# Block-sparse attention and a gated MLP in one kernel: scores by 512 and 256 columns, and five preparation steps moved to later slots

## The chip, the cores and the metric

The kernel runs on one core of a Trainium2 chip. The core has five engines with instruction streams of their own: TensorE (PE in the profile; its weight loads are PEld) for matrix products and transposes, VectorE (DVE), ScalarE (ACT), GpSimd (POOL) and SyncE (SP), which here issues DMAs. Each engine works through its stream in order and waits at semaphores. TensorE writes to PSUM, eight banks of 2 KB in each partition; GpSimd doesn't read PSUM in this kernel. The metric is the device time of one execution in microseconds, the median over runs.

## The reference

Attention over 4 batches, 8 heads, 768 positions and 64 dimensions a head, with a mask of 24 x 24 blocks of 32 positions (a band, the first and last row and column of blocks, and three sampled blocks in each row), then a gated MLP on the joined heads:

```python
scores = scale * np.matmul(q, k.transpose(0, 1, 3, 2))
...
scores = np.where(mask, scores, -1000000000.0)
scores = scores - np.max(scores, axis=-1, keepdims=True)
attn = np.exp(scores)
attn = attn / (np.sum(attn, axis=-1, keepdims=True) + 1e-09)
return np.matmul(attn, v).astype(np.float32)
...
h = np.maximum(x @ w_in, 0.0)
u, v = (h[..., :d_ff // 2].copy(), h[..., d_ff // 2:].copy())
...
v_n = (v - mu) / np.sqrt(var + 1e-06)
v_s = np.einsum('ts,bsd->btd', w_spatial, v_n) + b_spatial[None, :, None]
gated = u * v_s
return (gated @ w_out).astype(np.float32)
```

Here `x` is 4 x 768 x 512, `w_in` 512 x 1024, `w_spatial` 768 x 768 and `w_out` 512 x 512. The inputs are float32; the kernel computes its products in bfloat16.

## The kernel before

*The mask inside the product.* The tile `kq` holds, for eight heads at a time, K transposed (columns 0 to 767) and Q transposed (columns 768 to 1535) in partitions 0 to 63. Partitions 64 to 87 (`MR`) hold 24 block rows: on the K side a one where the column belongs to that block, on the Q side 0 or a large negative number for each (block, query). One product over 88 partitions gives score plus mask, transposed: keys in partitions, queries in columns. `mask_rows` makes the Q-side block rows for one third of the queries (256 columns) by a product of `bm` with the K-side rows of head 0 and a copy into head 0's rows; `rows` copies the rows of head 0 to other heads.

*Slots.* The program is written as a list of slots (`for s in range(NS + LAG + 2)`), and the engines' streams follow that order; nothing is reordered later. Each slot issues one score tile of 128 keys (four parts for a unit) with its exponential on ScalarE, into one of two PSUM tiles `sc` of two banks each. Then come the functions of `pre`, the products of the exponentials with V that are due (tags `av`, two banks), the functions of `at`, some steps of the MLP from a queue (`run_queue`), and the functions of `late`.

Slots 0 to 35 (batch 0) work in units of a third of the queries and a pair of heads (`qk_unit`, L395 and L400; `av_unit`, L441), so that work can begin before all of Q is there. Heads 0 and 1 come first with two thirds at once, then pairs 1 to 3 with the first third, pairs 1 to 3 with the second (from slots 15, 18 and 21 on), and all four pairs with the last (from slots 24, 27, 30 and 33 on). Slots 36 to 179 (batches 1 to 3) take one head and one tile of 128 keys against all 768 queries (`qk_full`, L408 and L412; `av_full`, L459).

*Preparation for batch 0.* K and Q arrive in natural layout, are cast by GpSimd, and are transposed on TensorE (L261) into a PSUM bank, from which VectorE copies them into `kq` (L209). `tr_first(p)` does K and the first third of Q for pair p; `tr_rest(p)` the rest of Q: four transposes and two copies of 64x512. The block rows of heads 1 to 7 are copies of `rows` on VectorE or GpSimd (L239). All of these hang in the slots' lists; `ROWS` names slot, first head, last head and columns for those on VectorE.

*The shared banks.* Two single PSUM banks, `moeA` and `moeB`, are handed out in turn by `moe_tag`: to `mask_rows`, to `tr_first` and `tr_rest`, to the transposes of the attention's result for pair 0 (`xtr_third(1)`, at the end of slot 13), and to each product of the MLP. A user of a bank can start when the copy out of it by the user before the last has ended. The MLP of batch 0 begins at slot 16 (`open_first`): one step, a product of 512 columns (L545), and keeps that bank until slot 20. The results of the other units are transposed into the unused end of their own `av` tile (`xtr_third`, at slots 14, 15, 19 and so on), and copied out to `xt`; the tile can then be used for the unit after the next.

*GpSimd* works through the casts of the inputs and weights (L135, L225) in the order of `ORDER`, which stands in its stream ahead of all slots; `rows(slice(1, 4), qcols(2), PL)` of slot 16 follows.

Of the kernel before, what the change touches and what calls it, by code (L numbers as in the profile page):

```python
# [10 lines left out]
FP32 = mybir.dt.float32  # L11
BF16 = mybir.dt.bfloat16
I32 = mybir.dt.int32
AF = mybir.ActivationFunctionType
# [12 lines left out]
def kernel(  # L27
# [16 lines left out]
    nc = tc.nc  # L44

    B, H, S, D = q.shape
# [4 lines left out]
    HALF = S // 2  # L51
# [19 lines left out]
    psum = ctx.enter_context(tc.tile_pool(name="psum", bufs=1, space=bass.MemoryType.PSUM))  # L71
# [10 lines left out]
    kq = const.tile([KR, H, 2 * S], BF16, name="kq")  # L82
# [5 lines left out]
    def qcols(t0, n=1):  # L88
        return slice(S + t0 * TW, S + (t0 + n) * TW)
# [144 lines left out]
    def rows(hs, cs, eng=nc.vector):  # L234
        src = kq[MR, 0:1, cs].to_broadcast([NB, hs.stop - hs.start, cs.stop - cs.start])
        if eng is nc.scalar:
            nc.scalar.activation(out=kq[MR, hs, cs], in_=src, func=AF.Copy)
        else:
            eng.tensor_copy(out=kq[MR, hs, cs], in_=src)  # L239
# [11 lines left out]
    def moe_tag():  # L251
        moe_tags.rotate(1)
        if moe_tags[0] in held:
            moe_tags.rotate(1)
        return moe_tags[0]
# [10 lines left out]
    def mask_rows(ps, t, copy, h=0):  # L266
        nc.tensor.matmul(out=ps[:, 0:TW], lhsT=bm, rhs=kq[:, h, t * TW:(t + 1) * TW],
                         start=True, stop=True)
        copy(kq[MR, 0, qcols(t)], ps[0:NB, 0:TW])
# [103 lines left out]
    a_ref, av_ref, x_ref, xn_ref, xt_ref = {}, {}, {}, {}, {}  # L373
# [28 lines left out]
    def qk_full(j, ci):  # L402
        if ci == 0:
            a_ref["h", j] = work.tile([128, NCH * S], BF16, tag="a_all", bufs=3,
                                      name="a_all").rearrange("p (c n) -> p c n", c=NCH)
        ps = psum.tile([128, 1024], FP32, tag="sc", bufs=2)
        for hf in range(2):
            nc.tensor.matmul(out=ps[:, hf * 512:hf * 512 + HALF],  # L408
                             lhsT=kq[:, j % H, ci * 128:(ci + 1) * 128],
                             rhs=kq[:, j % H, S + hf * HALF:S + (hf + 1) * HALF],  # L410
                             start=True, stop=True)
        nc.scalar.activation(  # L412
            out=a_ref["h", j][:, ci, :].rearrange("p (b c) -> p b c", b=2),
            in_=ps.rearrange("p (b c) -> p b c", b=2)[:, :, 0:HALF], func=AF.Exp, scale=0.125)

    def av_tile(key, n):
        ps = psum.tile([128, 512], FP32, tag="av", bufs=2, name="ps_av")
# [277 lines left out]
    at, late, pre = {}, {}, {}  # L695

    def when(slot, *fns):
        at.setdefault(slot, []).extend(fns)

    def c(f, *a, **kw):  # L700
        return lambda: f(*a, **kw)

    K_Q0 = slice(0, S + TW)
    ROWS = [(3, 2, 8, qcols(0)), (1, 3, 4, K_), (4, 4, 6, K_), (8, 6, 8, K_),
            (14, 4, 8, qcols(1, 2))]
    when(0, second)
    when(1, third)
    when(2, lambda: filler(FILL3, psum.tile([128, 512], FP32, tag=moe_tag(), bufs=1, name="wps")))
# [1 line left out]
        when(sl, c(tr_first, p))  # L710
    for sl, h0, h1, cs in ROWS:
        when(sl, c(rows, slice(h0, h1), cs))
    when(3, lambda: mask_rows(psum.tile([128, 512], FP32, tag=moe_tag(), bufs=1, name="mq"), 2, dve_copy))
    when(16, lambda: rows(slice(1, 4), qcols(2), PL))
    for p, sl in ((1, 11), (2, 13), (3, 15), (0, 18)):
        when(sl, c(tr_rest, p, 2 if p == 0 else 1))
    for u, slot in enumerate((13, 14, 15, 19, 22, 25, 28, 30, 34, 37, 40), 1):
        (pre if u == 2 else late).setdefault(slot, []).append(c(xtr_third, u))
# [94 lines left out]
    for s in range(NS + LAG + 2):  # L813
        if s < S0:
            qk_unit(*divmod(s, 3))
        elif s < NS:
            j, ci = divmod(s - S0, NCH)
            qk_full(j + H, ci)
        early = at.get(s, [])
        for f in pre.get(s, []):  # L820
            f()
        for u, e in av_at.get(s, []):
            av_unit(u, e)
        if 0 <= s - LAG - S0 and s - LAG < NS:
            j, qc = divmod(s - LAG - S0, NCH)
            av_full(j + H, qc)
        for f in early:
            f()
        run_queue()
        for f in late.get(s, []):  # L830
            f()
        while post:
            post.pop(0)()
# [31 lines left out]
```

## Time and profile before

| | us |
|---|---|
| median of 3 runs | 211.86 (211.82 to 212.51) |
| the profiled execution | 211.45 |
| its span, first to last instruction | 209.4 |
| TensorE busy | 203.5 (97%) |
| ScalarE busy | 168.7 (81%) |
| VectorE busy | 131.5 (63%) |
| GpSimd busy | 85.0 (41%) |

A row of a timeline gives the start, the duration, the engine, the line, and the operation with what it writes and reads, and in brackets the idle time of the engine before it and what ended that. Rows of one line that follow each other are merged (x4). A matmul's duration has a tail in it that lies under the next one, so for TensorE the distance from start to start is the cost, and a wait can hide in a duration. A row of busy time by stretch gives the stretch, its length, then for PE, PEld, DVE, ACT and POOL the busy time and the number of instructions, the granted clock of TensorE, the mean share of the DMA engines and GB/s.

### The profile page before, as it was taken

The numbers are of one execution on the slowest core, as the hardware profiler recorded it, in microseconds if no ns is written. First come the engines' busy times: TensorE is split into PE (matmuls) and PEld (weight loads), VectorE is DVE, ScalarE is ACT, GpSimd is POOL, SyncE is SP. The second block draws the span as 40 slices with busy tenths as digits, with TensorE's granted clock in tenths as the row PEclk, the third lists the DMA queues.
The fourth block names the chain that finished last, engine by engine and source line by source line (L and its number), as shares of the span: only waits on it lengthen the run. The fifth ranks groups of instructions, "written<-read, shape, count | busy, mean of one in ns | idle before, by whom it ended". The sixth has DMA issues, their size and how long they took to land.

```text
span 209.4 us, 5342 instructions
## 1 busy us (share of the span) xinstructions
PE 203.5 (97%) x2140; PEld 129.3 (62%) x2140; DVE 131.5 (63%) x292; ACT 168.7 (81%) x221; POOL 85.0 (41%) x184
## 2 busy tenths in 40 slices
PE   7899999999999999999999999999999999999993
PEld 6698877756666666656555665565665556544441
DVE  7899776989654455594965464284984443476551
ACT  6999999999989999978898888989899787266021
POOL 7888869886919615007068061006220000012000
PEclk9999999999999999999999999999999999999999
DMA  5999899999999989689955697488401225510256
GB/s 156 349 360 349 272 328 271 240 315 354 277 305 191 280 239 250 227 212 366 172 186 113 153 220 170 173 187 254 83 3 38 50 53 121 214 56 2 50 146 229
DMA packets 64684, 41.96 MB, mean 200 GB/s; under 512 B 45716, under 2 KB 59412, under 8 KB 64660
## 3 DMA queue, kind: packets, MB, share of 16 engines
q1 hardware_dynamic: 64228, 41.24, 75.8%
q10 hardware_dynamic: 432, 0.39, 0.6%
q8 instruction: 16, 0.26, 0.5%
q14 instruction: 8, 0.07, 0.1%
HBM read 24.38 MB, written 6.29 MB: 146 GB/s over the span
## 4 chain that ended last, share of the span: by engine, by line
PE 90%; ACT 5%; DMA 2%; DVE 1%; issue 0%; ACTq 0%; POOL 0%
PE ps_moe L545 33%; PE ps L408 22%; PE ps_av L459 13%; PE ps_t L545 7%; PE ps L395 5%; ACT a_all L400 4%; PE ps_av L441 4%; PE ps_sc L545 3%; DMA st_q<-in_q_dram 1%; DMA out_dram<-osb 1%; PE ps L261 1%; PE ps_av L261 1%; DVE kq L209 0%; ACT osb L212 0%; DVE xt L209 0%
## 5 line engine op out<-in xcount | busy, mean ns | idle before, releaser
L412 ACT ACTIVATE a_all<-ps 128x768 bf16<-128x768 f32 x144 | 113.8, 812 | 15.8 <-PE ps L408 7.2
L408 PE MATMUL ps<-kq 88*128 88x384 bf16 x288 | 70.5, 325 | 0.0
L459 PEld LDWEIGHTS <-a_all 128*128 128x128 bf16 x864 | 46.4, 97 | 20.0
L459 PE MATMUL ps_av<-vv,a_all 128*128 128x65 bf16 x864 | 51.2, 194 | 0.0
L408 PEld LDWEIGHTS <-kq 88*128 88x128 bf16 x288 | 28.0, 98 | 30.2 <-issue 0.2
L545 PE MATMUL ps_moe<-w_in_t,xt 128*128 128x512 bf16 x144 | 43.8, 378 | 0.0
L400 ACT ACTIVATE a_all<-ps 128x1024 bf16<-128x1024 f32 x36 | 34.6, 1027 | 1.1 <-PE ps L395 0.8
L135 POOL CAST nat<-st_k 128x256 bf16<-128x256 f32 (+3 forms) x37 | 16.6, 481 | 43.4 <-DMA st_k<-in_k_dram 30.6
L545 PE MATMUL ps_moe<-vn,w_spt 128*128 128x512 bf16 x108 | 32.7, 378 | 0.0
L613 DVE SCALAR_TENSOR_TENSOR un<-ps_moe,b_col,un 128x512 bf16<-128x512 f32 x18 | 13.5, 749 | 17.1 <-PE ps_moe L545 16.9
L582 POOL TENSOR_SCALAR std<-mv 128x3 f32<-128x3 f32 (+1 forms) x9 | 2.2, 240 | 50.3 <-DVE mv L579 37.0
L395 PE MATMUL ps<-kq 88*128 88x256 bf16 (+1 forms) x140 | 21.5, 275 | 1.0 <-ACT a_all L400 0.6
L545 PE MATMUL ps_moe<-w_out_t,gt 128*128 128x512 bf16 x72 | 21.5, 378 | 0.0
L423 DVE RECIPROCAL rc<-ps_av 128x6 f32<-128x6 f32 (+1 forms) x36 | 6.6, 185 | 20.7 <-PE ps_av L459 18.9
L135 POOL CAST vv<-st_v 128x256 bf16<-128x256 f32 (+1 forms) x36 | 18.1, 534 | 3.8 <-DMA st_v<-in_v_dram 3.8
L545 PEld LDWEIGHTS <-xt 128*128 128x128 bf16 x192 | 15.2, 97 | 7.0 <-DVE xt L209 0.2
L424 DVE TENSOR_TENSOR xn<-ps_av,rc 128x384 bf16<-128x384 f32 (+1 forms) x36 | 18.5, 513 | 1.2
L135 POOL CAST nat<-st_q 128x256 bf16<-128x256 f32 (+2 forms) x41 | 18.1, 472 | 0.9 <-DMA st_q<-in_q_dram 0.6
L578 DVE BATCH_NORM_STATS2 stats<-vn 128x6 f32<-128x512 bf16 x24 | 16.5, 688 | 1.5 <-ACT vn L573 0.9
L183 DVE TENSOR_SCALAR vn<-ps_moe 128x512 bf16<-128x512 f32 x18 | 12.3, 684 | 6.0 <-PE ps_moe L545 6.0
L395 PEld LDWEIGHTS <-kq 88*128 88x128 bf16 x140 | 12.6, 97 | 4.7 <-issue 0.9
L209 DVE COPY kq<-tt 64x1536 bf16<-64x1536 bf16 x24 | 14.9, 619 | 0.3
(86 smaller groups left out, 210.1 us busy)
## 6 DMA issues: line engine op xcount, KB each, us to landing
st_v<-in_v_dram SPq DMA_DIRECT2D x16, 384.0 KB, 6.0
out_dram<-osb SPq DMA_DIRECT2D x23, 256.0 KB, 2.4
st_k<-in_k_dram SPq DMA_DIRECT2D x15, 384.0 KB, 4.4
st_q<-in_q_dram SPq DMA_DIRECT2D x12, 384.0 KB, 4.2
ws_f<-in_moe_w_spatial_dram SPq DMA_DIRECT2D x6, 384.0 KB, 5.0
w_f<-in_moe_w_in_dram SPq DMA_DIRECT2D x8, 256.0 KB, 6.3
w_f<-in_moe_w_out_dram SPq DMA_DIRECT2D x4, 256.0 KB, 5.3
st_q<-in_q_dram SPq DMA_DIRECT2D x3, 256.0 KB, 6.6
```

What stands on the lines that cost most here:

```text
L135: eng.tensor_copy(out=dst, in_=src)
L183: nc.vector.tensor_scalar(out=out, in0=in0, scalar1=s1, scalar2=s2, op0=o0, **kw)
L209: nc.vector.tensor_copy(out=o, in_=i)
L395: nc.tensor.matmul(out=ps[:, at:at + n * TW], lhsT=kq[:, h, ci * 128:(ci + 1) * 128], rhs=kq[:, h, qcols(t0, n)], start=True, stop=True)
L400: nc.scalar.activation(out=out, in_=ps, func=AF.Exp, scale=0.125)
L408: nc.tensor.matmul(out=ps[:, hf * 512:hf * 512 + HALF], lhsT=kq[:, j % H, ci * 128:(ci + 1) * 128], rhs=kq[:, j % H, S + hf * HALF:S + (hf ...
L412: nc.scalar.activation(out=a_ref["h", j][:, ci, :].rearrange("p (b c) -> p b c", b=2), in_=ps.rearrange("p (b c) -> p b c", b=2)[:, :, 0:H ...
L424: nc.vector.tensor_tensor(out=out, in0=ps[:, :, 0:D], in1=rc[:, 0:n].to_broadcast([128, n, D]), op=ALU.mult)
L459: nc.tensor.matmul(out=av_ref[j][:, qc, :], lhsT=a_ref["h", j][:, ci, qc * 128:(qc + 1) * 128], rhs=vv[p % NVV][:, h, ci, :], start=(ci == ...
L545: nc.tensor.matmul(out=ref["ps"][:, 0:w], lhsT=lhs(i), rhs=rhs(i), start=(i == 0), stop=(i == n - 1))
L578: nc.vector.bn_stats(out=stats, in_=self.vn[:, tcc, :])
L613: nc.vector.scalar_tensor_tensor(out=self.un[:, tcc, :], in0=ps, scalar=b_col[:, tcc:tcc + 1], in1=self.un[:, tcc, :], op0=ALU.add, op1=AL ...
```

## The change

`qk_full` splits its 768 columns into 512 and 256 instead of two halves of 384 in two banks; the scores then lie next to each other in PSUM, and the exponential reads 768 columns in one run. Of the preparation for batch 0, the mask product for the last third of the queries goes from slot 3 to slot 16, directly ahead of the copy on GpSimd that uses it; pair 2's `tr_rest` goes from slot 13 to the end of slot 14, pair 3's from slot 15 to slot 16. The block rows of heads 4 to 7 for the second and the last third, one copy at slot 14, become three: heads 4 and 5, second third, at slot 14; heads 6 and 7, second third, at slot 17; heads 4 to 7, last third, at slot 20. At slot 16 the order is: mask product and copy, GpSimd's rows, pair 3's transposes, the first step of the MLP.

```diff
--- before.py
+++ after.py
@@ -404,14 +404,11 @@
             a_ref["h", j] = work.tile([128, NCH * S], BF16, tag="a_all", bufs=3,
                                       name="a_all").rearrange("p (c n) -> p c n", c=NCH)
         ps = psum.tile([128, 1024], FP32, tag="sc", bufs=2)
-        for hf in range(2):
-            nc.tensor.matmul(out=ps[:, hf * 512:hf * 512 + HALF],
+        for n0, n1 in ((0, 512), (512, S)):
+            nc.tensor.matmul(out=ps[:, n0:n1],
                              lhsT=kq[:, j % H, ci * 128:(ci + 1) * 128],
-                             rhs=kq[:, j % H, S + hf * HALF:S + (hf + 1) * HALF],
-                             start=True, stop=True)
-        nc.scalar.activation(
-            out=a_ref["h", j][:, ci, :].rearrange("p (b c) -> p b c", b=2),
-            in_=ps.rearrange("p (b c) -> p b c", b=2)[:, :, 0:HALF], func=AF.Exp, scale=0.125)
+                             rhs=kq[:, j % H, S + n0:S + n1], start=True, stop=True)
+        nc.scalar.activation(out=a_ref["h", j][:, ci, :], in_=ps[:, 0:S], func=AF.Exp, scale=0.125)
 
     def av_tile(key, n):
         ps = psum.tile([128, 512], FP32, tag="av", bufs=2, name="ps_av")
@@ -702,7 +699,7 @@
 
     K_Q0 = slice(0, S + TW)
     ROWS = [(3, 2, 8, qcols(0)), (1, 3, 4, K_), (4, 4, 6, K_), (8, 6, 8, K_),
-            (14, 4, 8, qcols(1, 2))]
+            (14, 4, 6, qcols(1)), (17, 6, 8, qcols(1)), (20, 4, 8, qcols(2))]
     when(0, second)
     when(1, third)
     when(2, lambda: filler(FILL3, psum.tile([128, 512], FP32, tag=moe_tag(), bufs=1, name="wps")))
@@ -710,9 +707,10 @@
         when(sl, c(tr_first, p))
     for sl, h0, h1, cs in ROWS:
         when(sl, c(rows, slice(h0, h1), cs))
-    when(3, lambda: mask_rows(psum.tile([128, 512], FP32, tag=moe_tag(), bufs=1, name="mq"), 2, dve_copy))
+    late.setdefault(14, []).append(c(tr_rest, 2))
+    when(16, lambda: mask_rows(psum.tile([128, 512], FP32, tag=moe_tag(), bufs=1, name="mq"), 2, dve_copy))
     when(16, lambda: rows(slice(1, 4), qcols(2), PL))
-    for p, sl in ((1, 11), (2, 13), (3, 15), (0, 18)):
+    for p, sl in ((1, 11), (3, 16), (0, 18)):
         when(sl, c(tr_rest, p, 2 if p == 0 else 1))
     for u, slot in enumerate((13, 14, 15, 19, 22, 25, 28, 30, 34, 37, 40), 1):
         (pre if u == 2 else late).setdefault(slot, []).append(c(xtr_third, u))
```

## The prediction

> **What bounds the kernel now.** I read the page's spans first, then busy time by stretch, then the waits, and last the timeline of each engine around the slots that the change touches.
>
> ```profile
> span 209.4 us, 5342 instructions
> PE 203.5 (97%) x2140; PEld 129.3 (62%) x2140; DVE 131.5 (63%) x292; ACT 168.7 (81%) x221; POOL 85.0 (41%) x184
> ...
> PE 90%; ACT 5%; DMA 2%; DVE 1%; issue 0%; ACTq 0%; POOL 0%
> ```
>
> ```profile
> 5.00:21.40 16.40, 15.23 (x229) 13.01 (x230) 14.79 (x34) 15.66 (x19) 13.87 (x23) 1.00 1.03 348
> 21.40:40.80 19.40, 19.40 (x275) 15.52 (x272) 14.70 (x40) 19.05 (x20) 16.83 (x26) 1.00 1.06 276
> 40.80:46.00 5.20, 5.20 (x52) 3.21 (x51) 4.63 (x11) 4.85 (x7) 3.40 (x9) 1.00 1.13 304
> 46.00:182.00 136.00, 136.00 (x1436) 82.99 (x1434) 79.13 (x163) 116.76 (x157) 44.96 (x105) 1.00 0.78 189
> ```
>
> From 21.4 us to 182 us TensorE never stops, at a granted clock of 1.00: a microsecond that it loses before 21.4 us cannot be made up later, since nothing later waits, and one that it saves there comes off the end. Before that VectorE has 14.79 us of work in 16.4 us. So the question is what the change does to TensorE's waits before about 22 us, and to the length of its stream afterwards. TensorE around slots 14 to 17 (their score products are the L395 rows at 18.48, 19.29, 20.76 and 21.67 us; their order is that of the program):
>
> ```profile
> 18.04 0.38 PE L261 MATMUL ps<-ident,nat 128*128 128x128 bf16 x4
> 18.26 0.39 PE L261 MATMUL ps<-ident,xn 128*128 128x128 bf16 x4
> 18.48 0.60 PE L395 MATMUL ps<-kq 88*128 88x256 bf16 x4
> 18.92 0.28 PE L261 MATMUL ps_av<-ident,xn 128*128 128x128 bf16 x2
> 19.04 0.41 PE L441 MATMUL ps_av<-vv,a_all 128*128 128x65 bf16 x8
> 19.29 0.60 PE L395 MATMUL ps<-kq 88*128 88x256 bf16 x4
> 20.09 0.43 PE L441 MATMUL ps_av<-vv,a_all 128*128 128x65 bf16 x8 [0.20 <-DVE xt L209]
> 20.35 0.39 PE L261 MATMUL ps<-ident,nat 128*128 128x128 bf16 x4
> ```
>
> The score products of slot 15 need 0.44 us of stream, so the next row could start at 19.73 us; it starts at 20.09. It waits for the copy `xt` of VectorE that frees its PSUM tile:
>
> ```profile
> 18.53 0.85 DVE L209 COPY kq<-ps 64x512 bf16<-64x512 bf16 x2
> 19.41 0.42 DVE L209 COPY xt<-ps 128x512 bf16<-128x512 bf16 x1
> 19.75 0.28 DVE L209 COPY xt<-ps_av 128x256 bf16<-128x256 bf16 x1
> ...
> 20.61 0.80 DVE L239 COPY kq<-kq 24x2048 bf16<-24x2048 bf16 x1
> 21.44 0.86 DVE L209 COPY kq<-ps 64x512 bf16<-64x512 bf16 x2
> 22.32 0.29 DVE L209 COPY xt<-ps_av 128x256 bf16<-128x256 bf16 x1
> ```
>
> The two copies at 18.53 us are pair 2's remaining transposes; they stand ahead of the `xt` that is waited for.
>
> **The change, part by part.**
>
> *Mask product out of slot 3.* One product of 256 columns (a quarter of 0.44, 0.11 us) and its copy (CAST kq<-mq, 9.25 us, 0.42 us). TensorE waited 0.28 us for ScalarE right behind the product, and VectorE waited for the transposes of pair 1 behind the copy (its next row starts at 9.75, when their last matmul has ended). Both are covered; removal gains 0. The two shared PSUM banks (`moeA`, `moeB`) swap roles until slot 13; each user's predecessor is long copied out (pair 1's transposes at 9.10 against copies that ended at 7.97), so 0 again.
>
> *Pair 2's transposes from slot 13 to the end of slot 14.* VectorE's `xt` copies come 0.8 us sooner: 18.53 to 18.95 and, behind its transposes, 19.07 to 19.35. Slot 15's wait goes: 0.36 us, and the 0.06 us wait at 20.57 with it, a gain of 0.42. ScalarE does not take it back: it starts an activation every 0.92 us, and slot 14's would end at 19.95, before TensorE asks for slot 16's scores at 20.12. What is late next is VectorE itself.
>
> *Slot 16, the new waits.* TensorE now does here: scores to 20.56 (0.44 from 20.12), products with V to 20.82, the mask product to 20.93, pair 3's four transposes (0.22), and the first step of the dense product (0.22). The last three take banks in turn: mask one, transposes the other, dense product the first again. So pair 3's transposes wait for the two copies of pair 2's, issued only at the end of slot 14, and the dense product waits for the copy of the mask. VectorE's queue from 19.35, with 0.03 us between instructions as in the rows: reciprocal 0.18 and product 0.42 (to 19.98), block rows of heads 4 and 5 (to 20.33, below), pair 2's copies 0.86 (to 21.22), `xt` 0.29 (to 21.54), the mask's copy 0.42 (to 21.98). TensorE follows a copy after 0.06 us (19.75 + 0.28 against 20.09). Its transposes start at 21.28 instead of 20.93, a wait of 0.35; they end at 21.50 and the dense step starts at 22.04, a wait of 0.54. Slot 17 starts at 22.26 instead of 21.67: **+0.59 us**. As a sum: 0.11 (mask product, now in the open) + 0.35 + 0.54 - 0.42 = 0.58. Everything else on TensorE is the same work up to that point.
>
> *Block rows in three pieces.* The one row for heads 4 to 7 took 0.80 us, 24x2048. No row shows 24x512 on VectorE; GpSimd casts run beside it:
>
> ```profile
> 20.25 0.62 POOL L225 CAST w_in_t<-w_f 128x512 bf16<-128x512 f32 x1
> ```
>
> ```profile
> 20.95 0.93 POOL L225 CAST w_in_t<-w_f 128x512 bf16<-128x512 f32 x1
> ```
>
> The cast of 20.25 ends at 20.87; the rows, started at 20.61, end at 21.41, 0.54 us later; and the next cast, 0.62 alone, takes 0.93. I read this as taking turns, at 0.54 us for 2048 elements, so 0.14 for 512. The new piece starts at 20.00 under the cast of 19.56 to 20.18 and ends at about 20.33. Bounds: 0.14 us with no cast in the way, 0.82 (the longest of these copies); the sum of slot 16 moves with it, 0.40 to 1.08. The other pieces come at slots 17 and 20, when `xt` copies have some 0.1 to 0.4 us in hand: at slot 20 it is 1024 elements, 0.27, plus the rest of a cast of 0.83. I take 0, and 0.5 us as the far bound. Their consumers are at slots 21 and 30.
> The Trainium skill's page SBUF — State Buffer, section Who interferes with whom, says that VectorE's two-port copies and GpSimd hold one port pair in turn, each for its whole instruction; the two rows agree. Without it, a quarter of 0.80 would give 0.20 for the piece and 0.44 for slot 16.
>
> *GpSimd and SP.* GpSimd's rows for heads 1 to 3 must follow the mask's copy at 21.98, and reached their turn at 24.96: nothing. No DMA is moved; no load waits for a moved step.
>
> *Scores by 512 and 256.* 144 slots, the same columns. Start to start in 46 to 182 us: 384 columns take 166 ns first and 162 second, 512 take 215, 256 take 108 behind their own kind (slots before 40 us). The first of a pair pays about 4 ns for following another shape. New pair 219 + 108 = 327 against 328. The first product with V behind 256 columns takes 34.3 ns against 32.8 behind 384. So +1.5 ns at most by row, 144 x 1.5 = **+0.2 us**; the other end is that the 4 ns vanish, -0.6. A weight load (97 ns) still fits under 256 columns. ScalarE's activation (812 ns) keeps its 768 elements and is not what TensorE waits for.
>
> **Sum:** 0.59 + 0.2 = 0.8 us on the profiled execution's 211.45 us (span 209.4 and 2.05 around it), 212.25. The median of the runs, 211.86, is 0.41 above it: 212.65.
>
> **Rivals.**
> 1. *VectorE is in time* (the other side): the old wait goes and neither new one comes. TensorE reaches the dense step at 21.15, so the mask's copy would have to end by 21.09 instead of 21.98. For: the piece of rows could be 0.2 shorter, and the chain has seven hand-overs. Against: 3.4 us of work from 18.53 on. It decides where that work is under 2.6 us for both waits to go, under 2.9 for no loss at slot 17. Time: 0.11 - 0.42 + 0.2 = -0.1, 211.75.
> 2. *The split pays*: the 4 ns at a change of shape belong to the 384 columns and go. 0.59 - 0.6 = 0: 211.85. For: nothing but that no 512-column score is in the trace. Against: the 256-column group pays the same 4 ns.
> 3. *The lateness spreads*: the pieces at slots 17 and 20 fall behind casts, and VectorE, 0.6 us later for what follows, holds `xt` at slots 22 to 24. 0.8 + 0.5, and 1.08 in place of 0.59: up to 213.6, likeliest 213.2.
>
> **How the numbers follow.** 0.3% (0.64 us) is about what a measurement of this kernel can tell from none. Forecast 0.62, its own range 212.2 to 213.0: of this 0.42 lie above 212.50. Rival 1 0.12, of which 0.03 faster; rival 2 0.13, of which 0.06 faster; rival 3 0.13, slower. Together slower 0.55, within 0.36, faster 0.09. The range for 8 in 10 reaches from rival 1, less a little for the lower end of the split, to rival 3: 211.5 to 213.4.
>
> **What would show it.** In the profile after: `ps_av` L441 of slot 15 starts with no wait; a wait of pair 3's transposes (L261) on `kq` copies and of the dense step (L545) on the mask's copy near 21 to 22 us, some 0.9 us together; L408's two forms at 382 and 272 ns with slots as long as before. Wrong if TensorE reaches slot 17 before 21.7 us, or if the stretch of full slots changes length by over 0.3 us.

## The result, and the profile after

The changed kernel takes 212.97 us (median of 15 runs, 212.27 to 214.20) against 212.21 us for the kernel before in as many runs: a ratio of 1.0041, 95% interval 1.0025 to 1.0057, which is +0.5 to +1.2 us. The forecast was +0.8 us, slower.

The page of the kernel after, its span, engines and chain. The profiled execution took 213.62 us, 0.65 above its median, where that of before (211.45) lay 0.76 below its own, so the two spans differ by more than the kernels do:

```profile
span 211.3 us, 5311 instructions
PE 202.6 (96%) x2106; PEld 129.7 (61%) x2140; DVE 131.9 (62%) x294; ACT 168.7 (80%) x221; POOL 84.4 (40%) x184
...
PE 84%; DMA 7%; POOL 3%; DVE 1%; SPq 1%; issue 1%; ACT 0%; ACTq 0%
```

The work of the engines is that of before; 34 matmul records fewer are in this trace though no matmul was taken out, and TensorE's busy time is 0.9 us less with them. To keep executions apart from kernels, I cut each trace at the starts of the activations of a_all of slots 12, 18, 36 and 179, which ScalarE starts right behind each slot's scores:

| us | slot 12 starts at | 12 to 18 | 18 to 36 | 36 to 179 | 179 to the end |
|---|---|---|---|---|---|
| before | 17.09 | 6.19 | 17.93 | 135.05 | 33.13 |
| after | 18.18 | 7.00 | 17.94 | 135.05 | 33.14 |

The stretch with the moved steps is 0.81 us longer; from slot 18 on the two agree within 0.02 us, also in the 144 slots with the new split. The 1.1 us before slot 12 is most likely not the change's: in this execution TensorE waited 0.37 us for a GpSimd cast in front of pair 1's transposes, work of which nothing was moved. The first experiment, with the order of before in these slots, starts slot 12 at 17.95, later by 0.86 too. Over all eleven profiles of this document, slot 12 starts at 17.98 us on average in the four with the mask product at slot 16, and at 17.96 in the seven with it at slot 3.

TensorE after, timeline of slots 14 to 17 (their scores are the L395 rows at 19.35, 20.38, 21.19 and 23.57 us; L542 is L545 of before):

```profile
19.35 0.60 PE L395 MATMUL ps<-kq 88*128 88x256 bf16 x4
19.79 0.28 PE L261 MATMUL ps_av<-ident,xn 128*128 128x128 bf16 x2
19.91 0.41 PE L438 MATMUL ps_av<-vv,a_all 128*128 128x65 bf16 x8
20.16 0.39 PE L261 MATMUL ps<-ident,nat 128*128 128x128 bf16 x4
20.38 0.60 PE L395 MATMUL ps<-kq 88*128 88x256 bf16 x4
20.82 0.42 PE L438 MATMUL ps_av<-vv,a_all 128*128 128x65 bf16 x8
...
21.89 0.27 PE L267 MATMUL mq<-kq,bm 88*128 88x256 bf16 x1
22.67 0.38 PE L261 MATMUL ps<-ident,nat 128*128 128x128 bf16 x4 [0.50 <-DVE kq L209]
23.35 0.39 PE L542 MATMUL ps_moe<-w_in_t,xt 128*128 128x512 bf16 x1 [0.30 <-POOL w_in_t L225]
23.57 0.38 PE L395 MATMUL ps<-kq 88*128 88x256 bf16 x2
```

Slot 15's products with V follow its scores after 0.44 us: the old wait is gone. The two new ones stand at 22.67 and 23.35. From start to start, less what the instruction in front streams (0.11 for the mask product, 0.055 for a transpose), they are 0.67 and 0.46 us. The second is put down to GpSimd, one of whose weight casts happened to end at 23.33; the cast that this step reads is the first of them, and had ended at 20.95. VectorE's line shows what came last:

```profile
21.04 0.62 DVE L239 COPY kq<-kq 24x512 bf16<-24x512 bf16 x1
21.66 0.85 DVE L209 COPY kq<-ps 64x512 bf16<-64x512 bf16 x2
22.55 0.29 DVE L209 COPY xt<-ps_av 128x256 bf16<-128x256 bf16 x1
22.87 0.42 DVE L209 CAST kq<-mq 24x256 bf16<-24x256 f32 x1
```

Block rows, pair 2's copies, `xt`, the mask's copy, without a gap; pair 3's transposes start 0.15 us after the copies end (22.52), the dense step 0.06 after the mask's copy (23.29). Sum: 0.11 + 0.67 + 0.46 - 0.42 = 0.82 us, the 0.81 of the table.

### The profile page after: what moved, and what is told of

Same layout as the page of the kernel before. It is cut to its first block, busy times and chain, and to the rows that moved or that the text cites. A ratio compares the mean times of both kernels' runs of the same rounds, so it can differ in the third digit from the quotient of the medians.

```text
span 211.3 us, 5311 instructions
## 1 busy us (share of the span) xinstructions
PE 202.6 (96%) x2106; PEld 129.7 (61%) x2140; DVE 131.9 (62%) x294; ACT 168.7 (80%) x221; POOL 84.4 (40%) x184
## 4 chain that ended last, share of the span: by engine, by line
PE 84%; DMA 7%; POOL 3%; DVE 1%; SPq 1%; issue 1%; ACT 0%; ACTq 0%
PE ps_moe L542 31%; PE ps L408 22%; PE ps_av L456 13%; PE ps_t L542 7%; DMA st_v<-in_v_dram 6%; PE ps L395 4%; PE ps_sc L542 3%; PE ps_av L438 3%; POOL w_in_t L225 1%; SPq L107 1%; DMA out_dram<-osb 1%; POOL vv L135 1%; PE ps_av L261 1%; DVE kq L209 0%; ACT osb L212 0%
## 5 line engine op out<-in xcount | busy, mean ns | idle before, releaser
L408 PE MATMUL ps<-kq 88*128 88x512 bf16 (+1 forms) x288 | 70.5, 325 | 0.2
L456 PE MATMUL ps_av<-vv,a_all 128*128 128x65 bf16 x864 | 51.2, 194 | 0.1
L542 PE MATMUL ps_moe<-w_in_t,xt 128*128 128x512 bf16 x128 | 39.4, 378 | 0.8 <-POOL w_in_t L225 0.3
L542 PE MATMUL ps_moe<-vn,w_spt 128*128 128x512 bf16 x98 | 30.5, 378 | 0.6
L395 PE MATMUL ps<-kq 88*128 88x256 bf16 (+1 forms) x140 | 21.6, 275 | 1.1 <-ACT a_all L400 0.5
L542 PE MATMUL ps_moe<-w_out_t,gt 128*128 128x512 bf16 x66 | 20.2, 378 | 0.1
L542 PEld LDWEIGHTS <-xt 128*128 128x128 bf16 x192 | 15.2, 97 | 7.5 <-DVE kq L209 0.5
L395 PEld LDWEIGHTS <-kq 88*128 88x128 bf16 x140 | 12.6, 97 | 4.6 <-issue 1.0
L438 PE MATMUL ps_av<-vv,a_all 128*128 128x65 bf16 x288 | 14.8, 194 | 0.0
```

Source lines behind the costliest of these rows:

```text
L395: nc.tensor.matmul(out=ps[:, at:at + n * TW], lhsT=kq[:, h, ci * 128:(ci + 1) * 128], rhs=kq[:, h, qcols(t0, n)], start=True, stop=True)
L408: nc.tensor.matmul(out=ps[:, n0:n1], lhsT=kq[:, j % H, ci * 128:(ci + 1) * 128], rhs=kq[:, j % H, S + n0:S + n1], start=True, stop=True)
L438: nc.tensor.matmul(out=av_ref[u][:, to, :], lhsT=a_ref[u][:, at:at + 128], rhs=vv[pp % NVV][:, h, ci, :], start=(ci == 0), stop=(ci == NCH ...
L456: nc.tensor.matmul(out=av_ref[j][:, qc, :], lhsT=a_ref["h", j][:, ci, qc * 128:(qc + 1) * 128], rhs=vv[p % NVV][:, h, ci, :], start=(ci == ...
L542: nc.tensor.matmul(out=ref["ps"][:, 0:w], lhsT=lhs(i), rhs=rhs(i), start=(i == 0), stop=(i == n - 1))
```

## Experiments

Stretches and waits are from each run's own trace, cut as above; the ratios are to runs of the kernel before on the same chip.

### The split alone

```diff
 # the kernel before, with
-        for hf in range(2):
+        for n0, n1 in ((0, 512), (512, S)):
...
```

> Before, with only the scores split as 512 and 256 columns. Theory A (the loss sits in two bank waits at slot 16, the split is free): the full slots keep their length, 166 + 162 = 328 ns for a pair of before against 220 + 108 = 328 in the profile after; within 0.2 us of before, ratio 0.999 to 1.001. Rival B (the split costs or pays along all 144 slots): 0.2 us or more slower by 1.5 ns a slot, or 0.6 us faster by 4 ns a slot. Rival C (the loss is GpSimd's and the DMAs' early lateness, which the profile after shows as a wait of 0.54 us at 9.1 us, and the change causes it): no loss here.

211.88 us against 212.04, ratio 0.9996 (0.9979 to 1.0014). Start to start, the first score product of a slot takes 220 ns with 512 columns behind a dense step, the second 108, and the first product with V 33: 328 ns for the pair as before, and nothing for the products behind it. Slots 12 to 18 take 6.18 us and 18 to 36 17.93. The full slots took 135.31 in this execution, 0.26 more; one row holds it, a transpose of the MLP by DMA that landed late:

```profile
84.93 0.11 PEld L542 LDWEIGHTS <-gt 128*128 128x128 bf16 x2 [0.21 <-DMA gt<-un]
```

From start to start of the products around it this wait is 0.25 us. It isn't the split's: the kernel after has the same split and 135.05. Theory A stands and rival B falls by the products' starts; the interval of the time alone would leave room for 0.2 us. Rival C expected no loss here either. What speaks against it are the starts of slot 12, which show no lateness from the moved mask product, and the 0.81 us that the kernel after loses behind slot 12.

### The moves alone

```diff
 # the changed kernel, with
-        for n0, n1 in ((0, 512), (512, S)):
+        for hf in range(2):
...
```

> The changed kernel with the two halves of 384 columns put back, so the moves of the preparation alone. Theory A: all of the loss, +0.8 us by the profile after (0.11 of mask product + 0.67 + 0.46 of waits - 0.42 of the wait that goes), ratio 1.003 to 1.005; slot 12 to slot 17 longer by 0.8 us than before. Rival B: at most half of it, ratio under 1.002.

212.98 us, ratio 1.0042 (1.0022 to 1.0063): all of the loss. Slots 12 to 18 take 6.66 us in its trace, +0.47 and not the 0.8 expected; the profiled execution, 212.57, was also 0.41 below the median. The dense step waits 0.46 us as in the kernel after, pair 3's transposes 0.33 instead of 0.67, and that difference is the block rows':

```profile
20.62 0.28 DVE L239 COPY kq<-kq 24x512 bf16<-24x512 bf16 x1
20.92 0.86 DVE L209 COPY kq<-ps 64x512 bf16<-64x512 bf16 x2
21.81 0.29 DVE L209 COPY xt<-ps_av 128x256 bf16<-128x256 bf16 x1
22.13 0.42 DVE L209 CAST kq<-mq 24x256 bf16<-24x256 f32 x1
```

The same copy, 0.28 us here and 0.62 there: it depends on where a GpSimd cast stands. Here it began at 20.62, just behind the end of one cast and before the start of the next, and it is that next cast that took longer:

```profile
20.00 0.61 POOL L225 CAST w_in_t<-w_f 128x512 bf16<-128x512 f32 x1
20.67 0.71 POOL L225 CAST w_in_t<-w_f 128x512 bf16<-128x512 f32 x1
```

In the kernel after, a cast ran beside it:

```profile
20.90 0.61 POOL L225 CAST w_in_t<-w_f 128x512 bf16<-128x512 f32 x1
```

The copy, issued at 21.04, ends 0.14 us after that cast (21.51).

### The mask product back at slot 3

```diff
 # the changed kernel, with
-    when(16, lambda: mask_rows(psum.tile([128, 512], FP32, tag=moe_tag(), bufs=1, name="mq"), 2, dve_copy))
+    when(3, lambda: mask_rows(psum.tile([128, 512], FP32, tag=moe_tag(), bufs=1, name="mq"), 2, dve_copy))
```

> The changed kernel with the mask product of the last third back at slot 3; all else moved as in the change. Theory A: pair 3's transposes then take the bank of pair 0's, long copied out, and do not wait; the dense step takes pair 2's bank and waits for its copies, about 0.47 us; the mask's 0.11 is covered again. With the 0.42 that goes: +0.05 us against before, ratio 0.999 to 1.002, so about 0.8 us better than the changed kernel. Rival D (three pieces of block rows and a later VectorE make the loss, wherever the mask stands): still +0.5 us or more, ratio 1.0025 or more.

212.44 us, ratio 1.0018 (0.9999 to 1.0037): at the upper end of theory A's range, with an interval that reaches into rival D's. The trace says why. Slots 12 to 18 take 6.39 us, +0.20 and not +0.05: pair 3's transposes don't wait, and the dense step waits for pair 2's copies, but 0.65 us instead of 0.47, since the rows ahead of those copies took 0.71 here instead of 0.62, and the step started 0.15 us after the copies' end and not 0.06. Slots 18 to 36 take 18.45, +0.52, in one wait at slot 24:

```profile
27.11 1.09 DVE L239 COPY kq<-kq 24x1024 bf16<-24x1024 bf16 x1
28.23 0.69 DVE L183 TENSOR_SCALAR vn<-ps_moe 128x512 bf16<-128x512 f32 x1
28.96 0.69 DVE L575 BATCH_NORM_STATS2 stats<-vn 128x6 f32<-128x512 bf16 x1
29.69 0.18 DVE L576 BATCH_NORM_AGGREGATE mv<-stats 128x2 f32<-128x6 f32 x1
29.79 0.66 DVE L183 TENSOR_SCALAR vn<-ps_moe 128x512 bf16<-128x512 f32 x1
30.36 0.28 DVE L209 COPY xt<-ps_av 128x256 bf16<-128x256 bf16 x1
```

```profile
29.73 0.60 PE L395 MATMUL ps<-kq 88*128 88x256 bf16 x4
30.70 0.38 PE L438 MATMUL ps_av<-vv,a_all 128*128 128x65 bf16 x7 [0.36 <-DVE xt L209]
```

The piece of slot 20 met casts and took 1.09 us, where the kernel after had 0.42; what follows it on VectorE, `xt` at the end, came 0.5 us late. So in these traces the mask's place is part of the loss, and the pieces of rows are another part when they meet a cast.

### Only pair 2's transposes later

```diff
 # the kernel before, with
-            (14, 4, 8, qcols(1, 2))]
+            (15, 4, 8, qcols(1, 2))]
...
-    for p, sl in ((1, 11), (2, 13), (3, 15), (0, 18)):
+    for p, sl in ((1, 11), (3, 15), (0, 18)):
...
+    late.setdefault(14, []).append(c(tr_rest, 2))
```

> Before, with only pair 2's remaining transposes at the end of slot 14, and the one copy of block rows of heads 4 to 7 at slot 15, behind their copies. The mask stays at slot 3 and pair 3's transposes at slot 15. Theory A: the wait of 0.36 us at slot 15 goes and the small one of 0.06 behind it; the dense step takes pair 2's bank at 21.04 us, and pair 2's copies, with no rows ahead of them, end at 20.87, so no wait takes their place: -0.4 us, ratio 0.998 (0.997 to 0.9995), faster than both kernels. Rival E (VectorE is full here, any order of its work makes TensorE wait as long): within 0.1 us of before, a wait elsewhere in slots 15 to 18.

211.93 us, ratio 1.0003 (0.9982 to 1.0025): above theory A's 0.997 to 0.9995 and within rival E's 0.1 us, though the interval covers both. The trace has the gain where it was expected: slots 12 to 18 take 5.75 us, -0.44, and the dense step doesn't wait. Slots 18 to 36 take 18.07, +0.14, a wait at slot 18 for an `xt` copy that now stands behind the whole copy of rows (0.76 us) and pair 3's copies. So rival E is right about a wait that comes up elsewhere, though not about its size. What is left in the trace, 0.3 us, is less than the interval can tell.

### The rows behind pair 2's copies

```diff
 # the changed kernel, with
-            (14, 4, 6, qcols(1)), (17, 6, 8, qcols(1)), (20, 4, 8, qcols(2))]
+            (17, 6, 8, qcols(1)), (20, 4, 8, qcols(2))]
...
     late.setdefault(14, []).append(c(tr_rest, 2))
+    late[14].append(c(rows, slice(4, 6), qcols(1)))
```

> The changed kernel with the block rows of heads 4 and 5 (second third) issued behind pair 2's copies at the end of slot 14 instead of ahead of them. Theory A (what counts is when the mask's copy, last in VectorE's line, is done): the wait moves and does not shrink. Pair 3's transposes wait 0.05 us or less instead of 0.34 to 0.67, the dense step waits 0.8 to 1.2 us instead of 0.46; activation of slot 12 to that of slot 18 stays 0.5 to 0.8 us longer than the 6.18 us of before. Rival F (each bank wait is its own, and the first one is what the rows cost): the first wait goes and the second stays at 0.46; the stretch is 0.3 to 0.6 us shorter than the changed kernel's.

212.77 us in a single run, and in its trace the wait has moved and not shrunk:

```profile
21.52 0.27 PE L267 MATMUL mq<-kq,bm 88*128 88x256 bf16 x1
21.63 0.39 PE L261 MATMUL ps<-ident,nat 128*128 128x128 bf16 x4
22.88 0.39 PE L542 MATMUL ps_moe<-w_in_t,xt 128*128 128x512 bf16 x1 [0.86 <-DVE kq L209]
```

Pair 3's transposes follow the mask product at once; the dense step waits 1.02 us from start to start. Slots 12 to 18 take 6.90 us, +0.71. Rival F falls: what counts is the end of the last copy in VectorE's line.

### The rows on ScalarE

```diff
 # the changed kernel, with
-            (14, 4, 6, qcols(1)), (17, 6, 8, qcols(1)), (20, 4, 8, qcols(2))]
+            (17, 6, 8, qcols(1)), (20, 4, 8, qcols(2))]
...
+    when(14, c(rows, slice(4, 6), qcols(1), nc.scalar))
     late.setdefault(14, []).append(c(tr_rest, 2))
```

> The changed kernel with that same piece of rows on ScalarE instead of VectorE. Theory A: VectorE's line is shorter by the piece, 0.28 to 0.71 us by the profiles; the first wait goes, the dense step waits about 0.5 us; slot 12 to slot 18 is +0.2 us against before (6.4 us), 0.25 to 0.6 better than the changed kernel. ScalarE starts slot 15's activation 0.6 us later, which no score product waits for. Rival G (ScalarE is the limit here): slot 16's or 17's scores wait 0.3 us or more for an activation, and the stretch stays at 6.7 us or more.

212.37 us in a single run. The first wait is gone, the second is 0.45 us, and no score product of these slots waits for an activation.

```profile
21.85 0.27 PE L267 MATMUL mq<-kq,bm 88*128 88x256 bf16 x1
21.97 0.39 PE L261 MATMUL ps<-ident,nat 128*128 128x128 bf16 x4
22.64 0.39 PE L542 MATMUL ps_moe<-w_in_t,xt 128*128 128x512 bf16 x1 [0.28 <-DVE kq L209]
```

```profile
20.88 0.85 DVE L209 COPY kq<-ps 64x512 bf16<-64x512 bf16 x2
21.76 0.29 DVE L209 COPY xt<-ps_av 128x256 bf16<-128x256 bf16 x1
22.16 0.42 DVE L209 CAST kq<-mq 24x256 bf16<-24x256 f32 x1
```

Slots 12 to 18 take 6.32 us, +0.13, and 0.11 + 0.45 - 0.42 is 0.14. That is 0.68 us less than in the kernel after, where the piece took 0.62 of VectorE, and 0.34 less than with the moves alone, where it took 0.28: VectorE's line is priced about one to one. (The 0.68 us are a little more than the 0.6 that theory A allowed.) Theory A stands, rival G falls. One part of the loss is not VectorE's to give back: before the mask's copy VectorE stands idle for 0.11 us here (22.05 to 22.16), because the mask product itself has only just ended (21.85 + 0.27). The 0.45 us that is left is that copy, 0.42, between two users of one bank.

### A version for both: rows in two pieces

```diff
 # the kernel before, with
-            (14, 4, 8, qcols(1, 2))]
+            (16, 4, 8, qcols(1)), (25, 4, 8, qcols(2))]
...
-    for p, sl in ((1, 11), (2, 13), (3, 15), (0, 18)):
+    for p, sl in ((1, 11), (3, 16), (0, 18)):
...
+    late.setdefault(14, []).append(c(tr_rest, 2))
```

> Before, with pair 2's transposes at the end of slot 14, pair 3's at slot 16, and the block rows of heads 4 to 7 in two pieces, second third at slot 16, last third at slot 25, where VectorE is idle; the mask stays at slot 3. Theory A: the wait of slot 15 goes (0.42 us with the small one), the dense step at slot 16 finds pair 2's copies just ended, and nothing large stands ahead of the xt copies: slot 12 to slot 18 5.75 us, slot 18 to 36 17.94, so -0.4 us, ratio 0.998 (0.9965 to 1.0). Rival E (VectorE's fullness moves the wait elsewhere, as 0.15 us at slot 18 in the kernel before this one): -0.2 us or less, ratio 0.999 to 1.001.

The trace is as expected, slots 15 to 17 without a wait (scores of slot 15 at 19.82, of slot 17 at 21.77):

```profile
20.26 0.42 PE L441 MATMUL ps_av<-vv,a_all 128*128 128x65 bf16 x8
20.52 0.27 PE L261 MATMUL ps_av<-ident,xn 128*128 128x128 bf16 x2
20.63 0.60 PE L395 MATMUL ps<-kq 88*128 88x256 bf16 x4
21.07 0.42 PE L441 MATMUL ps_av<-vv,a_all 128*128 128x65 bf16 x8
21.33 0.39 PE L261 MATMUL ps<-ident,nat 128*128 128x128 bf16 x4
21.55 0.38 PE L545 MATMUL ps_moe<-w_in_t,xt 128*128 128x512 bf16 x1
21.77 0.60 PE L395 MATMUL ps<-kq 88*128 88x256 bf16 x4
```

Slots 12 to 18 take 5.75 us and 18 to 36 17.93. But the time was 211.95 against 211.91, ratio 0.9998 (0.9980 to 1.0017). In the profiled execution 0.39 us went again in the full slots (135.44), 0.35 of it in one wait for VectorE at 105.7 us. The same kernel twice more, both against the same 22 runs of before:

> The kernel of e6_two_pieces a second time, for more runs, because its interval of 0.2% to either side cannot tell -0.4 us from nothing. Theory A, that the 0.43 us saved up to slot 18 reaches the end: ratio 0.998. Rival H, that it is given back where single executions wait in the full slots (0.25 us at 84.7 us in e1_split, 0.35 us at 105.7 us in e6_two_pieces): 0.9995 to 1.0005. In the profile: slot 12 to slot 18 5.75 us again; slot 36 to the last score product 135.05 us without such a wait.

> The same kernel a third time, for the same reason and with the same numbers: ratio 0.998 by theory A, 0.9995 to 1.0005 by rival H.

211.57 and 211.70 us against 212.04: ratios 0.9983 (0.9961 to 1.0005) and 0.9984 (0.9964 to 1.0004). Both traces have 5.75 us from slot 12 to 18, 17.94 and 17.95 to slot 36, and 135.05 to slot 179. Taken together, over two chips, 36 runs have a median of 211.83 against 211.95 in 39 runs of before. The 0.44 us in the stretch are shown by four traces (that with only pair 2's transposes moved included); that they come off the time is likely and not shown, since each interval reaches 1.0. By the ratios to before (0.998 to 1.000 against 1.004) it is about 1 us faster than the changed kernel.

## Why the prediction was right

*Direction and size.* Forecast +0.8 us, measured +0.5 to +1.2 (ratio 1.0041). By its steps: slot 16 was put at +0.59; the profiles of the whole change and of the moves alone have +0.81 and +0.47. The split was put at +0.2 and costs 0.0. The two misses nearly cancel in the sum, so that it came out within 0.1 us is luck; that it is a loss, and where it arises, is not.

*The mask product out of slot 3, gains 0.* Right: from the activation of slot 0 to that of slot 4 it is 3.64 us in the kernel before, in the kernel after and with the mask back at slot 3. From slot 12 on, the experiment with the mask back differs from the change only by slot 16's waits and a collision at slot 20.

*The old wait goes, 0.42.* Right. It is gone in the kernel after and in all runs that move pair 2's transposes; -0.44 us from slot 12 to 18 where no new wait comes.

*Two new waits for the banks.* Right in place, order and cause, 0.35 and 0.54 us against 0.67 and 0.46 in one trace and 0.33 and 0.46 in the other. The second was 0.08 too high, because the transposes ahead of it started 0.15 us after the copies that free their bank, not 0.06. The first is off by 0.32 in one trace: 0.29 for the rows (0.62 us, not 0.33), 0.09 for that later start, less 0.06 because VectorE reached the rows earlier than forecast. In the other trace the rows took 0.05 less than forecast, and the three nearly cancel.

*Rows piece, 0.33 us, between 0.14 and 0.82.* Within its bounds; as a value it lies in a gap of what came: the copy of 24x512 took 0.28, 0.62, 0.63 and 0.71 us in four traces. The lower bound is a misreading: 0.14 us is what the copy needs after a cast has ended, and with no cast in the way it took 0.28 (in the moves alone, and at slot 17 with the rows on ScalarE). So slot 16's low end, 0.40, is 0.54 by the prediction's own steps, and the 0.2 us that rival 1 hoped to save on this piece was at most 0.05. (By the same steps a piece of 0.20 us gives 0.46, not the 0.44 stated.) Under a cast the copy waits for the cast's end, as taken from the two casts of before: in the three traces with 0.62 to 0.71 us it ended 0.14 us after the cast. The Trainium skill's page SBUF — State Buffer, section Who interferes with whom, says so, and these rows agree.

*Rows at slots 17 and 20, 0, with 0.5 us as the far bound.* Right for the kernel after, and the far bound happened with the mask at slot 3: 1.09 us for 24x1024 and 0.53 us of wait at slot 24. That wait stood in one of the five traces of kernels that have this piece, so rival 3 was a possible execution, not the likely one.

*The split, +0.2.* The term that was mis-sized. The first product with V behind 256 columns costs 33 ns, as behind 384, not 34.3; the rows with 34.3 came from the first 40 us, where other products stood around them. The pair's 328 ns was foreseen to 1 ns, and rival 2, that the 4 ns at a change of shape vanish, is wrong: 512 columns pay them too (220 against 215).

*"Nothing later waits."* True of the profile of before, and not of every execution: waits of 0.25 and 0.35 us stood at 84.9 and 105.7 us in two others. Such a wait hides a small gain made early, as in the first trace of the last kernel; in the two others of it none came.

## What to carry to other kernels

Where two banks are handed out in turn, a step put between two users ties them together: price it by when the copy out of its bank ends in the copying engine's line, not by its own length. Where the copying engine's line is nearly full, a reordering can merely choose which wait comes last, so move the instruction that no one waits for behind those that someone does, and check what the last in line is. When executions scatter by more than the effect, cut the traces at fixed instructions and compare the stretch.

## What the runs showed that was not expected

- Eleven profiles of kernels with the same first twelve slots, or all but one product and its copy, start slot 12's activation between 17.09 and 18.62 us, with TensorE's waits there changing from trace to trace: for GpSimd's casts of loaded data, for VectorE's copies, for ScalarE. The runs of one kernel spread over 1.4 to 2.3 us where there are 12 or more; that this is the same scatter is likely and was not tried.
- The small copies of block rows on VectorE are priced by the cast beside them more than by their size: 24x512 in 0.28 to 0.72 us, 24x1024 in 0.42 to 1.09.
- TensorE restarted 0.06 us after the copy that it waited for in one place, and 0.15 us in another, where a wait instruction of 51 ns of the weight loads stood ahead of the transposes (or, with the mask back at slot 3, of the dense step). That this instruction makes the difference is not shown.
